# Two decoder layers on one core: projection weights fetched again, sums on VectorE, halos issued after turnings, the seventh chunk by seven products

## The chip, the core and the metric

One of the eight NeuronCores of a Trainium2 chip runs the whole program. The metric is the device time of one execution in microseconds (us). Engines: PE is TensorE (matmul), PEld its weight load, DVE is VectorE, ACT is ScalarE, POOL is GpSimd, SP is SyncE, which only issues DMAs here. All five run their own instruction list strictly in the order in which it was written.

## The reference, cut to what matters

```python
def _A_ref(x, wqkv, wo):             # attention: 32 heads of 18, window 8, dilation 2
    qkv = (x @ wqkv) -> q, k, v
    idx = pos[:, None] - arange(8) * 2           # keys s, s-2, ..., s-14
    logits = einsum("bhsd,bhswd->bhsw", q, k[idx]) * 18 ** -0.5     # masked where idx < 0
    return einsum("bhsw,bhswd->bhsd", softmax(logits), v[idx]) @ wo
def _B_ref(x, w1, w2):               # feed-forward, 576 -> 4608 -> 576
    return silu(x @ w1) @ w2
x = A_x                              # 2048 tokens x 576, f32
for _ in range(2):                   # the same weights in both layers
    x = x + _A_ref(layernorm(x), A_wqkv, A_wo)
    x = x + _B_ref(layernorm(x), B_w1, B_w2)
```

## The kernel before, in words

**Chunks.** The 2048 tokens are cut into four chunks of 512, and with two layers there are eight steps s = 0 to 7, "chunk s" below; chunks 4 to 7 are the second layer, and the seventh chunk is s = 6. Every f32 operand of a matmul is held as two f16 halves (high and low), so a product takes three matmuls. In the feed-forward, chunks 0 and 1 are computed plainly (`ffn`), chunks 2 to 7 in pairs of 128-row weight blocks (`ffn_pairs`): 18 pairs q, in six groups g of three.

**A pair.** Its first product x @ w1 is a 2x2 block product done with seven block products P1 to P7 instead of eight (`product`, L1199, seven matmuls of 128x256 each). For these the inputs are combined beforehand: `forms` makes sums of blocks of x (L1153), splits them (L1162 to L1168) and turns them by DMA transposes into `xf` (L1172). ACT and DVE take the results out of the four PSUM banks and add them up (L1203, L1206, L1226), and Silu follows. The second product with w2 is done in one of two ways. `second` (L1316) does it plainly: 48 matmuls of 128x288 a pair. `seconds` (L1289) does it by seven block products: 42 matmuls a pair. For these `hidden_forms` makes four sums a pair (L1253, on POOL) and splits them (L1258, L1261), and the weights must have been combined before by `prepare_second` (two loads L1095, four sums L1101 on POOL, a split on ACT L1103 and DVE L1104, a store L1106), once for each of the 18 pairs. `TWICE` says from which group on a chunk uses `seconds`: chunk 6 from group 2, chunk 7 from group 0.

**Attention of the second layer.** For each chunk, four units u of 8 heads: a load of wqkv's part (`load_wq`, 1080 KB, one buffer), 4 x 14 matmuls (L717), evacuation by ACT (L784, L786), and then the "halo": four DMAs on POOL's queue that copy the last rows of keys and values to the neighbour partition (L798). DVE computes scores and weighted sums (L818, L822, L851, L858). `project` then handles the chunk's four 128-token tiles j: DVE splits o, SP issues a DMA transpose ("turning", L496, `yo<-yh`, two buffers `yo`), PE multiplies by wo (L894, 28 matmuls), DVE adds the residual in place (L905) and POOL's queue writes it out (`xe<-o`, L899). `turn` later loads it again and makes the chunk's `forms`.

**Order.** The order of every instruction list is made when the program is built. The class `Plan` holds the operations with an assumed duration, a priority (`prio`, lower first), their dependencies (`after` adds some by hand) and their buffers; `order` plays them through with assumed DMA times (1.2 us before, 0.9 us after, and a rate) and writes each engine's list in the order in which that play started them. `AT`, `AN` and `AD` are priorities of the second layer's attention, so that its work lies among the matmuls of the chunk before. What the chip does when a DMA or an engine is later than in that play is wait.

**Areas.** `area` and `part` lay several kinds of tiles over the same bytes of SBUF; a tile can be taken when nothing that overlaps it is alive. The weights `wo` have a tile of their own throughout. The four sums `turn` makes of each half of a chunk (`ye`, `yd`) lie in the area of `xa` (turned normalized inputs of attention) or, for chunk 5, of `o` (attention's output).

## Time and profile before

| | |
|---|---|
| three runs, us | 2153.5, 2153.89, 2156.87; median 2153.89 |
| the profiled execution, us | 2151.35 |
| its span, first to last instruction, us | 2149.6 |
| PE busy | 2101.2 us, 98% |
| DVE, ACT, POOL busy | 1730.4 us (81%), 1014.7 us (47%), 540.6 us (25%) |
| granted clock of TensorE, mean | 0.996 |
| DMA | 482.00 MB, 224 GB/s |

A row of the windows view gives for a stretch of time the busy us of each engine with its number of instructions, the granted clock of TensorE, the busy share of the 16 DMA engines and GB/s. A row of the waits view gives who waited for whom: us in total, how often, the longest. A row of the chain or the timeline gives start, length and what ran; the timeline adds in brackets how long the engine had been idle before and who ended that. The chain's rows on a DMA run from its issue to its landing.

### The profile page before, as it was taken

What the parts mean: (1) busy time and instruction counts of PE and PEld (TensorE: products, weight loads), DVE (VectorE), ACT (ScalarE), POOL (GpSimd) and SP (SyncE); (2) the same over time, 40 slices, a digit from 0 to 9 for tenths busy, and PEclk for the clock granted to TensorE, in tenths of its full rate; (3) what the DMA queues carried; (4) which work ended last, traced back from release to release, by engine and by line L of the source; (5) the groups of instructions that cost most, each with busy time, mean ns of one, the idle gap of its engine ahead of it and who ended that gap; (6) DMA issues with size and microseconds to landing.
All of it is one profiled execution on the core that took longest, in us unless ns stands there. A gap on an engine that the chain in (4) does not pass through costs nothing.

```text
span 2149.6 us, 41975 instructions
## 1 busy us (share of the span) xinstructions
PE 2101.2 (98%) x16053; PEld 1560.2 (73%) x16053; DVE 1730.4 (81%) x2681; ACT 1014.7 (47%) x1851; POOL 540.6 (25%) x819
## 2 busy tenths in 40 slices
PE   8999899999999999999999999999999999999999
PEld 5556466655667888777777867778787887887887
DVE  8999999999978999789989968974997457555444
ACT  7555788654344553344324424424444454444443
POOL 2224656243332230111101000010002624222222
PEclk9999999999999999999999999999999999999999
DMA  6577777697889987687668986787769897979772
GB/s 181 156 224 253 253 259 252 171 273 250 230 200 285 323 260 217 165 249 194 172 190 206 268 204 194 212 185 201 221 174 252 308 294 243 281 205 270 209 208 76
DMA packets 372881, 482.00 MB, mean 224 GB/s; under 512 B 150072, under 2 KB 294820, under 8 KB 368712
## 3 DMA queue, kind: packets, MB, share of 16 engines
q1 hardware_dynamic: 327848, 331.25, 55.4%
q0 software_dynamic: 42816, 146.97, 21.2%
q8 instruction: 125, 2.05, 0.4%
q10 hardware_dynamic: 2016, 1.11, 0.2%
q14 instruction: 76, 0.62, 0.1%
HBM read 345.36 MB, written 85.37 MB: 200 GB/s over the span
## 4 chain that ended last, share of the span: by engine, by line
PE 79%; DMA 9%; DVE 7%; issue 3%; ACT 1%; POOL 1%; SPq 0%; ACTq 0%; DVEq 0%; POOLq 0%
PE acc L1316 19%; PE misc L1199 12%; PE z L1199 12%; PE z L717 8%; PE acc L1289 7%; PE z L1358 7%; PE acc L1377 6%; PE misc L717 5%; PE acc L894 4%; DMA yo<-yh 2%; DMA w<-w2s 1%; DMA w<-wfs 1%; DMA wq<-in_B_w_dram 1%; DVE xa L1067 1%; DVE x L905 1%
## 5 line engine op out<-in xcount | busy, mean ns | idle before, releaser
L1199 PEld LDWEIGHTS <-w 128*128 128x128 f16 x5292 | 517.8, 98 | 87.8 <-issue 11.6
L1316 PE MATMUL acc<-w,h 128*128 128x288 f16 x3744 | 484.0, 286 | 0.0
L1316 PEld LDWEIGHTS <-h 128*128 128x128 f16 x3744 | 366.1, 98 | 89.1
L1199 PE MATMUL misc<-xb,w 128*128 128x256 f16 x2639 | 338.5, 273 | 10.9 <-DMA w<-wfs 4.4
L1199 PE MATMUL z<-xb,w 128*128 128x256 f16 x2653 | 338.3, 273 | 4.2 <-ACT wq L1203 3.0
L1377 PE MATMUL acc<-w,h 128*128 128x288 f16 x1728 | 215.8, 286 | 2.2 <-DMA w<-w2s 2.2
L717 PEld LDWEIGHTS <-xa 128*128 128x128 f16 x1344 | 131.3, 98 | 116.9 <-issue 4.1
L1377 PEld LDWEIGHTS <-h 128*128 128x128 f16 x1728 | 168.4, 98 | 46.8 <-issue 2.6
L851 DVE TENSOR_TENSOR prs<-kvs,pe 128x1152 f32<-128x1152 f32 x128 | 169.9, 1350 | 0.8
L818 DVE TENSOR_TENSOR prs<-qts,kvs 128x2304 f32<-128x2304 f32 x64 | 163.2, 2550 | 4.0 <-DMA kvs<-kvs 3.0
L822 DVE TENSOR_REDUCE lg<-prs 128x128 f32<-128x2304 f32 x64 | 162.9, 2546 | 1.0
L905 DVE SCALAR_TENSOR_TENSOR x<-acc,d,x 128x576 f32<-128x576 f32 x144 | 116.4, 811 | 54.8 <-PE acc L1316 48.6
L858 DVE TENSOR_TENSOR prs<-prs 128x1152 f32<-128x1152 f32 (+1 forms) x128 | 135.0, 1055 | 3.2
L1358 PE MATMUL z<-xb,w 128*128 128x512 f16 x588 | 129.1, 379 | 4.3 <-ACT w L978 1.6
L1298 DVE SCALAR_TENSOR_TENSOR x<-acc,d2x,x 128x576 f32<-128x576 f32 (+1 forms) x71 | 57.3, 809 | 86.1 <-PE acc L1289 83.7
L894 PE MATMUL acc<-wo,yo 128*128 128x288 f16 x896 | 117.0, 291 | 8.7 <-DMA yo<-yh 7.3
L717 PE MATMUL z<-wq,xa 128*128 128x432 f16 x630 | 121.7, 349 | 2.9 <-DMA wq<-wqs 2.9
L894 PEld LDWEIGHTS <-yo 128*128 128x128 f16 x896 | 88.6, 99 | 35.4 <-DMA yo<-yh 9.2
L1358 PEld LDWEIGHTS <-w 128*128 128x128 f16 x588 | 57.2, 98 | 73.5 <-DVE w L980 2.9
L717 PE MATMUL misc<-wq,xa 128*128 128x432 f16 x546 | 105.0, 346 | 2.7 <-ACT xa L494 1.3
L798 POOL DMA_DIRECT2D kvs<-kvs x64 | 34.5, 545 | 271.3 <-ACT qts L786 271.3
L1358 PE MATMUL z<-xb,wq 128*128 128x512 f16 x420 | 94.5, 384 | 2.6 <-ACT h L1360 2.6
(302 smaller groups left out, 3227.3 us busy)
## 6 DMA issues: line engine op xcount, KB each, us to landing
w<-wfs SPq DMA_DIRECT2D x756, 160.0 KB
w<-w2s SPq DMA_DIRECT2D x192, 288.0 KB
wq<-wqs SPq DMA_DIRECT2D x17, 1080.0 KB
kvs<-kd POOLq DMA_DIRECT2D x8, 1584.0 KB, 10.3
w<-w1s SPq DMA_DIRECT2D x36, 320.0 KB
wfs<-xa POOLq DMA_DIRECT2D x18, 640.0 KB, 4.6
w2s<-w POOLq DMA_DIRECT2D x36, 288.0 KB, 4.2
kvs<-wts SPq DMA_DIRECT2D x67, 144.0 KB
```

The source lines that it names most:

```text
L717: nc.tensor.matmul(T(m)[:, :3 * UC], a, b, start=n == 0, stop=n == len(pl) - 1)
L818: nc.vector.tensor_tensor(T(pr), T(qt)[:, j:j + 2, None, :].to_broadcast([P, 2, W, UC]), win(T(kv), j, 2), op=ALU.mult)
L822: nc.vector.tensor_reduce(T(lg)[:, j:j + 2].rearrange("p a w h -> p (a w h)"), T(pr).rearrange("p a w (h d) -> p (a w h) d", d=DH), axis=A ...
L851: nc.vector.tensor_tensor(T(pr)[:, a].rearrange("p w (h d) -> p w h d", d=DH), v, T(pe)[:, j + a, :, :, None].to_broadcast([P, W, UH, DH]) ...
L858: nc.vector.tensor_tensor(t[:, :, 0:h, :], t[:, :, 0:h, :], t[:, :, h:2 * h, :], op=ALU.add)
L894: nc.tensor.matmul(T(acc)[:, h, 0:288], a, b[:, h * 288:(h + 1) * 288], start=n == 0, stop=n == len(pl) - 1)
L905: nc.vector.scalar_tensor_tensor(t, acc[:, :, 0:288], d, t, op0=ALU.mult, op1=ALU.add)
L1199: nc.tensor.matmul(t, w[:, u, :], v[:, r, :], start=first and m == 0, stop=m == 6, skip_group_check=True)
L1289: nc.tensor.matmul(T(acc)[:, j, 0:KH], T(hb[t])[:, a, row[k], j * P:(j + 1) * P], T(wb[k, t])[:, w, :], start=k in (5, 1, 2) and t == 0 an ...
L1316: nc.tensor.matmul(T(acc)[:, h, 0:288], T(hb[t])[:, a, f, j * P:(j + 1) * P], T(wbs[t][f])[:, h, w, :], start=t == 0 and f == 0 and m == 0 ...
L1358: nc.tensor.matmul(T(z), v, u, start=m == 0, stop=m == len(pl) - 1)
L1377: nc.tensor.matmul(T(acc)[:, h, 0:288], T(hb[q])[:, a, j * P:(j + 1) * P], T(wbs[q][0])[:, h, w, :], start=q == 0 and m == 0, stop=q == n ...
```

## The change

- `TWICE` has 0 for chunk 6: all its 18 pairs use `seconds`.
- The sums of `hidden_forms` and `prepare_second` go from POOL to DVE, with new assumed durations.
- The tile of `wo` becomes the area `wos`, which the sums `ye` share; `yd` is gone. The split weights are stored to memory once (in step 2), and fetched again (1440 KB, `load_wo`) for the projections of chunks 5 and 6, and again for that of chunk 7. Four dependencies by hand that kept `xa`, `o` and the sums apart go away.
- `free`: unit 1's matmuls and edges of chunks 5 to 7 must follow the last turning of the projection before, so its halo comes behind the turnings.
- `lag`: the planner takes it that matmuls of `project` (2.5 us) and of `product` (0.7 us) in the second layer can start so much after the DMA that they need.

```diff
-TWICE = {6: 2, 7: 0}
+TWICE = {6: 0, 7: 0}
+LAGP = 2.5
+LAGX = 0.7
...
-                t = max(t, d.end + (0.0 if d.eng == o.eng and not d.nbytes else self.LAT))
+                t = max(t, d.end + (0.0 if d.eng == o.eng and not d.nbytes else self.LAT) + (o.lag if d.nbytes else 0.0))
...
-    part("ye", XA, 1, [2, 4, KH], F32)
-    part("yd", O, 1, [2, 4, KH], F32)
-    tag("wo", 1, [P, 10, D], F16)
+    WOA = area("wos", 10 * D * 2)
+    part("wo", WOA, 1, [10, D], F16)
+    part("ye", WOA, 1, [2, 4, KH], F32)
...
+    def load_wo(prio):
+        w = Buf("wo")
+        op("SP", 0.41, lambda: nc.sync.dma_start(fl(T(w)), wos), ["wos"], [(w, k) for k in range(10)], prio, nbytes=P * 20 * D, after=formed[-1:])
+        return w
...
         for u in range(NU):
+            free = held[:1] + (flipped[-1:] if s > NC and u == 1 else [])
...
-                    op("SP", 0.8, edge, [("eds", lay, par, u)], [(kv, "edge")], pr_, nbytes=20000, lanes=2, after=held[:1])
+                    op("SP", 0.8, edge, [("eds", lay, par, u)], [(kv, "edge")], pr_, nbytes=20000, lanes=2, after=free)
...
-                           [m, (kv, "hold")] if lay else [m], pr_, after=held[:1])
+                           [m, (kv, "hold")] if lay else [m], pr_, after=free)
...
-                    op("DVE", 1.28, mul, keys + [pe], [(pr, a)], pd, after=formed[-1:] if s <= NC or s == NC + 3 else ())
+                    op("DVE", 1.28, mul, keys + [pe], [(pr, a)], pd, after=formed[-1:] if s <= NC else ())
...
-            transposed(oh, lambda oT=oT: T(oT), oT, j, pd, s < 2)
+            flipped.append(transposed(oh, lambda oT=oT: T(oT), oT, j, pd, s < 2))
...
-            op("PE", 3.43, mm, [(oT, j)] + [(WO, k) for k in range(10)], [acc], pr_)
+            op("PE", 3.43, mm, [(oT, j)] + [(w, k) for k in range(10)], [acc], pr_, lag=LAGP if s >= NC else 0.0)
...
-                nc.gpsimd.tensor_tensor(t[:, r], t[:, x], t[:, y], op=ALU.subtract)
-        op("POOL", 3.8, sums, [(b, 0)], [(b, 0)], prio)
+                nc.vector.tensor_tensor(t[:, r], t[:, x], t[:, y], op=ALU.subtract)
+        op("DVE", 1.85, sums, [(b, 0)], [(b, 0)], prio)
...
-                    return op("PE", 0.763, mm, [wf[k], (xf[k], 0), (xf[k], 1)], [z], pp + 0.01 * q)
+                    return op("PE", 0.763, mm, [wf[k], (xf[k], 0), (xf[k], 1)], [z], pp + 0.01 * q, lag=LAGX if s >= NC else 0.0)
...
-            op("POOL", 0.75, lambda hq=hq, r=r, u=u, v=v, o=o: nc.gpsimd.tensor_tensor(T(hq)[:, r], T(hq)[:, u], T(hq)[:, v], op=o),
+            op("DVE", 0.42, lambda hq=hq, r=r, u=u, v=v, o=o: nc.vector.tensor_tensor(T(hq)[:, r], T(hq)[:, u], T(hq)[:, v], op=o),
...
-                   [(yh, 0), (yh, 1), (xT, "hold")], p, nbytes=P * 9 * P * 2, after=formed[-1:] if s == NC + 2 else ())
+                   [(yh, 0), (yh, 1), (xT, "hold")], p, nbytes=P * 9 * P * 2)
...
     def attend(s):
-        project(s, attention(s, normed[s], lambda u: load_wq(u, AT[s], "wz")))
+        if s in (NC + 1, NC + 3):
+            outs.append(load_wo(AT[s]))
+        project(s, attention(s, normed[s], lambda u: load_wq(u, AT[s], "wz")), None, outs[-1])
 
     def turn(s):
-        XT[s] = forms(load_x(s, s - 1.0, spilt=True), s - 1.0, late=spilled[-1:] if s == NC + 1 else gate[-1:], into="yd" if s == NC + 1 else "ye")
+        XT[s] = forms(load_x(s, s - 1.0, spilt=True), s - 1.0, into="ye")
...
+        if s == 2:
+            op("POOL", 0.55, lambda: nc.gpsimd.dma_start(wos, fl(T(WO))), [(WO, k) for k in range(10)], ["wos"], 2.0, nbytes=P * 20 * D, after=attended[-1:])
```

Since the plan is played through anew, the lists differ from the third chunk (s = 2) on; up to there they are the same but for names. PE has 36 matmuls fewer. Three places follow; line numbers of the changed kernel are up to 10 higher (L496 is now L500, L663 L667, L798 L808, L887 L897, L899 L909, L915 L925, L1077 L1087, L1104 L1114).

**SP, the projection of chunk 6.** Before (L496 `yo<-yh` are the four turnings, L887 the residuals' loads, L663 a unit's weights, L1077 weights of `product`):

```order
L887 DMA o<-xd_110 128x576
L496 DMA_TRANSPOSE yo<-yh 128x9x128
L887 DMA o<-xd_111 128x576
L496 DMA_TRANSPOSE yo<-yh 128x9x128
L663 DMA wq<-wqs_252 128x4320
L887 DMA o<-xd_112 128x576
L496 DMA_TRANSPOSE yo<-yh 128x9x128
L887 DMA o<-xd_113 128x576
L496 DMA_TRANSPOSE yo<-yh 128x9x128
```

With the change:

```order
L897 DMA o<-xd_110 128x576
L500 DMA_TRANSPOSE yo<-yh 128x9x128
L1087 DMA w_70<-wfs_228 128x640
L897 DMA o<-xd_111 128x576
L500 DMA_TRANSPOSE yo<-yh 128x9x128
L1087 DMA w_70<-wfs_228 128x640 x2
L1087 DMA w_70<-wfs_229 128x640
L897 DMA o<-xd_112 128x576
L1087 DMA w_70<-wfs_229 128x640 x2
L500 DMA_TRANSPOSE yo<-yh 128x9x128
L897 DMA o<-xd_113 128x576
L500 DMA_TRANSPOSE yo<-yh 128x9x128
```

The load of the next unit's weights, which is issued when the matmuls of the unit before are done, stood between the second and the third turning; now all four turnings come first.

**POOL, the projection of chunk 5.** Before (L899 `xe<-o` writes out a projected tile, L798 is a halo's four DMAs):

```order
L899 DMA xe_122<-o 128x576
L899 DMA xe_123<-o 128x576
L899 DMA xe_124<-o 128x576
L798 DMA kvs<-kvs 112x1152
L798 DMA kvs<-kvs 15x1152
L798 DMA kvs<-kvs 112x864
L798 DMA kvs<-kvs 14x864
L899 DMA xe_125<-o 128x576
```

With the change:

```order
L909 DMA xe_122<-o 128x576
L909 DMA xe_123<-o 128x576
L909 DMA xe_124<-o 128x576
L909 DMA xe_125<-o 128x576
L808 DMA kvs<-kvs 112x1152
L808 DMA kvs<-kvs 15x1152
L808 DMA kvs<-kvs 112x864
L808 DMA kvs<-kvs 14x864
```

The halo of unit 1 of chunk 6 follows the last projected tile of chunk 5; the halo of unit 0 still stands ahead of `xe_122`, but the matmuls that it waits for come earlier on PE: between unit 0's last matmul and the projection's first stood 12 matmuls, and now 248.

**The sums of `prepare_second`.** Before, on POOL:

```order
L1101 TENSOR_TENSOR kvs<-kvs 128x288 x8
L1101 TENSOR_TENSOR prs<-prs 128x288 x4
L1106 DMA wts_232<-kvs 128x2304
L1106 DMA wts_233<-kvs 128x2304
L899 DMA xe_130<-o 128x576
```

With the change, on DVE (L1111 are the sums, L1114 the split, L915 the residual adds of L905 before):

```order
L1111 TENSOR_TENSOR kvs<-kvs 128x288 x4
L915 SCALAR_TENSOR_TENSOR o<-acc_98,so,o 128x576
L1111 TENSOR_TENSOR kvs<-kvs 128x288 x4
L1114 SCALAR_TENSOR_TENSOR kvs<-kvs,accw 128x4x288
L915 SCALAR_TENSOR_TENSOR x_75<-acc_99,d_307,x_75 128x576
L1114 SCALAR_TENSOR_TENSOR kvs<-kvs,accw 128x4x288
```

POOL has no arithmetic left there; DVE's list has the sums between its other work. On PE the projection of chunk 7 stands among the products of chunk 5's pairs 4 to 6 instead of its pairs 11 to 14, and in chunk 6 the first matmuls of `seconds` follow the last of chunk 5's `second`.

More of the change, by code (lines that the diff above doesn't have):

```diff
@@ L65 @@
 class Op:
-    __slots__ = ("eng", "dur", "fn", "prio", "seq", "deps", "outs", "n", "bufs", "nbytes", "start", "end", "table", "lanes")
+    __slots__ = ("eng", "dur", "fn", "prio", "seq", "deps", "outs", "n", "bufs", "nbytes", "start", "end", "table", "lanes", "lag")
 class Plan:
@@ L86, in slots, with op @@
         self.named[tag] = 0
-    def op(self, eng, dur, fn, reads=(), writes=(), prio=0.0, nbytes=0, table=None, after=(), lanes=1):
+    def op(self, eng, dur, fn, reads=(), writes=(), prio=0.0, nbytes=0, table=None, after=(), lanes=1, lag=0.0):
         o = Op()
+        o.lag = lag
         o.eng, o.dur, o.fn, o.prio, o.seq, o.nbytes, o.table = eng, dur, fn, prio, len(self.ops), nbytes, table
@@ L399, in sliding_attention_silu_ffn @@
     wts = [tc.dram_tile([P, 4 * 2 * KH], F16, name=f"wts{q}") for q in range(NP)]
+    wos = tc.dram_tile([P, 10 * D], F16, name="wosd")
     wqs = [tc.dram_tile([P, 30 * UC], F16, name=f"wqs{u}") for u in range(NU)]
@@ L507, in sliding_attention_silu_ffn @@
     attended, spilled, stored = [], [], []
-    turned, held = [], []
+    turned, held, flipped = [], [], []
     marks = []
@@ L770, in clear @@
                         nc.gpsimd.memset(T(kv)[0:1, 3:7], 0.0)
-                    op("POOL", 1.86, clear, [], [(kv, "edge")], pr_, after=held[:1])
+                    op("POOL", 1.86, clear, [], [(kv, "edge")], pr_, after=free)
                 else:
@@ L859, in tree @@
                     nc.vector.tensor_tensor(T(o)[:, j:j + 2, u * UC:(u + 1) * UC], t[:, :, 0, :], t[:, :, 1, :], op=ALU.add)
-                done = op("DVE", 2.55, tree, [], [(pr, 0), (pr, 1), (o, j, u), (o, j + 1, u)], pd, after=formed[-1:] if s <= NC or s == NC + 3 else ())
+                done = op("DVE", 2.55, tree, [], [(pr, 0), (pr, 1), (o, j, u), (o, j + 1, u)], pd, after=formed[-1:] if s <= NC else ())
                 if s == 0:
@@ L865, in attention, with project @@
         return o
-    def project(s, o, xs=None):
+    def project(s, o, xs=None, w=WO):
         pr_, pd = AT.get(s, s - 1.0), AD.get(s, s - 1.0)
@@ L887, in project @@
                 op("SP", 0.41, lambda j=j: nc.sync.dma_start(T(o)[:, j, :], xd[c][j]), [("xd", c, j)], src, pd, nbytes=P * D * 4)
-            transposed(oh, lambda oT=oT: T(oT), oT, j, pd, s < 2)
+            flipped.append(transposed(oh, lambda oT=oT: T(oT), oT, j, pd, s < 2))
             def mm(oT=oT, acc=acc):
-                pl = list(passes(lambda k: T(oT)[:, k, :], lambda k: T(WO)[:, k, :]))
+                pl = list(passes(lambda k: T(oT)[:, k, :], lambda k: T(w)[:, k, :]))
                 for n, (a, b) in enumerate(pl):
@@ L1459, in front @@
         XT[s] = layer_norm(X[s], s - 1.0, "xb", s == 1, s == 0) if s < S2 else forms(X[s], s - 1.0, ("ya", "yc"))
-    normed = {}
+    normed, outs = {}, [WO]
     def norm(s):
```

## The prediction

> **What bounds the kernel now.** I read the page first, then PE's waits, then stretches engine by engine, then the chain of waits around the longest gaps. The page's head:
>
> ```profile
> span 2149.6 us, 41975 instructions
> PE 2101.2 (98%) x16053; PEld 1560.2 (73%) x16053; DVE 1730.4 (81%) x2681; ACT 1014.7 (47%) x1851; POOL 540.6 (25%) x819
> ```
>
> PE is the bound: only 48.4 us of the span are not matmuls. So a change can gain in two ways, by fewer matmuls or by fewer gaps. The largest rows of PE's waits from 718 us to the end, in the part that the change reorders (up to about 580 us the lists are the same):
>
> ```profile
> PE acc L894 <- DMA yo<-yh: 7.3, 4, 2.9
> PE misc L1199 <- DMA w<-wfs: 4.4, 3, 3.5
> PE misc L1199 <- DVE wq L1206: 3.0, 2, 1.6
> PE z L1199 <- ACT wq L1203: 3.0, 2, 2.5
> PE z L717 <- DMA wq<-wqs: 2.9, 2, 2.7
> PE misc L1199 <- ACT wq L1203: 2.6, 3, 1.1
> ```
>
> That is 23.2 us in six rows. Most of the other idle time lies earlier and stays. A long gap costs twice, for after it the clock is lower. Windows right after gaps of 2.8, 1.5, 3.5, 2.5 and 2.9 us (PE, PEld, DVE, ACT, POOL, then the clock):
>
> ```profile
> 1436.20:1439.60 3.40, 3.40 (x16) 2.19 (x17) 0.88 (x1) 0.00 (x0) 0.00 (x0) 0.53 1.17 161
> 1087.40:1090.80 3.40, 3.40 (x29) 2.71 (x30) 0.59 (x1) 0.00 (x0) 0.00 (x0) 1.00 1.31 174
> 1977.20:1980.60 3.40, 3.39 (x29) 2.83 (x30) 0.63 (x2) 0.00 (x0) 0.32 (x1) 1.00 0.93 299
> 1804.60:1808.00 3.40, 3.40 (x19) 2.42 (x17) 3.40 (x10) 2.34 (x4) 0.38 (x1) 0.50 0.72 236
> 1275.20:1278.70 3.50, 3.50 (x17) 2.27 (x18) 3.46 (x4) 0.00 (x0) 0.00 (x0) 0.55 1.15 327
> ```
>
> After 1436 us 16 matmuls fit into 3.4 us where 29 fit after 1087 us: half the clock for 3.4 us, so 1.7 us lost on top of the gap.
>
> **The change part by part.**
>
> *Fewer matmuls.* Groups 0 and 1 of chunk 6 are six pairs; each needs 42 matmuls of 128x288 instead of 48, so 36 fewer. How fast they follow each other is in the chain of waits, which also has the turnings of the next part:
>
> ```profile
> 1050.11 5.88 PE acc L1316 x48
> 1072.26 3.43 PE acc L894 x28
> 1097.32 0.76 PE misc L1199 x7
> 831.47 7.22 DMA yo<-yh
> 1075.72 11.58 DMA yo<-yh
> 1258.65 16.47 DMA yo<-yh
> 1423.95 12.19 DMA yo<-yh
> 912.68 11.46 DMA wq<-wqs
> ```
>
> 5.88 / 48 = 0.1225 us, times 36: **-4.4 us**. PE is full in that stretch, so it counts.
>
> *Halos behind turnings.* Four turnings make one projection. One with no halo near it landed after 7.2 us; the three on which PE waited longest took 11.6, 16.5 and 12.2 us. Each time a halo was issued within 3 us of them on POOL's queue:
>
> ```profile
> 1073.09 2.12 POOL L798 DMA_DIRECT2D kvs<-kvs  x4 [11.83 <-ACT qts L786]
> 1259.08 2.13 POOL L798 DMA_DIRECT2D kvs<-kvs  x4 [14.93 <-ACT qts L786]
> 1421.02 2.11 POOL L798 DMA_DIRECT2D kvs<-kvs  x4 [21.52 <-ACT qts L786]
> DMA to landing us min/median/max: 4.5/9.3/13.8
> ```
>
> (The last row is of all halos: they move for 9.3 us.) What covers a turning can be counted. There are two `yo` buffers, so tile 2's turning is issued when tile 0's matmuls are done. In chunk 6's projection 28 matmuls of L894, 42 of L1199 and 12 of L1316 stood between those and tile 2's, which is 3.4 + 4.6 + 1.5 = 9.5 us; 12.2 less 9.5 is 2.7, and PE waited 2.8. In the changed list the covers of tile 2 in the four projections come to 10.8, 9.5, 9.4 and 9.4 us, about as before; but no halo and no unit's weight load stands among the turnings any more, so 7.2 us should do. Then the 7.3 us go, and with them the two spells at half the clock after 1275 and 1436 us: **-7.3 - 3.4 = -10.7 us**. The bounds: if only the halos of unit 1 were to blame (1073 and 1421 us), 1.5 + 2.8 + 1.7 = 6.0; if other transfers delay the turnings as much, nothing. I take the whole, since all three places are rid of both.
>
> The Trainium skill ("TensorE: Matmul & The Clock Gate", section "HAM oscillation — how this bites in real kernels") has it that only PE gaps above about 3.4 us are punished. By that the gaps of 2.8 and 2.9 us would cost no clock and this term would be -7.3. The rows above say otherwise in both directions: half the clock after 2.5 to 2.9 us, the full clock after 3.5.
>
> *Sums on DVE.* Most of the waits on L1203 and L1206 fall into the time from 1622 to 1818 us, in which POOL makes the sums of `prepare_second`. PE's waits from 1600 to 1810 us beside the row on L1206 above, one of them in the timeline, and one source line:
>
> ```profile
> PE z L1199 <- ACT wq L1203: 2.5, 1, 2.5
> PE misc L1199 <- ACT wq L1203: 2.1, 2, 1.1
> 1785.24 3.41 POOL L1101 TENSOR_TENSOR o<-o 128x288 f32<-128x288 f32 x4
> 1790.01 0.93 PE L1199 MATMUL misc<-xb,w 128*128 128x256 f16 x7 [1.63 <-DVE wq L1206]
> L522 DVE TENSOR_TENSOR nt<-nt x34: 160/161/646, 8.0 to 1787.2; 128x4 f32<-128x4 f32 x30, 128x2 f32<-128x2 f32 x4
> ```
>
> A step that takes 0.16 us elsewhere takes 0.65 on DVE at 1787 us, while POOL works; so DVE comes late to the adds in its list, PSUM banks stay full, and PE waits. With POOL's arithmetic gone DVE runs at its own pace: 3.0 + 2.5 + 2.1 and the spell after 1804 us, **-7.6 - 1.7 = -9.3 us**; the other bound is 0, if DVE is late by its own work. For it gets 72 sums of 128x288 and 144 of 128x256 (24 of them new, for the six pairs). Such a sum was not on DVE; its nearest rows are an add of that shape with one input in PSUM, 0.417 us, and POOL's own 0.725. I take the first, as the same engine's, and a ninth more for the larger, 0.46:
>
> ```profile
> L1206 DVE TENSOR_TENSOR wq<-misc,wq x90: 377/417/425, 923.0 to 2113.8; 128x256 f32<-128x256 f32 x90
> L1253 POOL TENSOR_TENSOR wq<-wq x80: 716/725/887, 1813.6 to 2117.4; 128x256 f32<-128x256 f32 x80
> 900.00:1550.00 650.00, 638.58 (x4964) 486.78 (x4963) 546.75 (x791) 252.89 (x499) 66.40 (x112) 0.99 0.78 210
> 1550.00:1850.00 300.00, 290.70 (x2455) 240.59 (x2454) 206.71 (x304) 132.68 (x240) 93.50 (x118) 0.99 0.83 248
> 1850.00:2145.00 295.00, 289.91 (x2497) 243.65 (x2496) 149.19 (x220) 125.12 (x227) 77.20 (x110) 1.00 0.71 205
> ```
>
> 72 x 0.46 + 144 x 0.417 = 93 us, all behind the attention of chunk 7 and so nearly all after 1550 us, where DVE has 93 + 146 = 239 us free: cost on the path 0. At POOL's price it would be some 160 us, which fits too.
>
> *Attention of chunk 7 earlier.* DVE has 103 us free between 900 and 1550 us. The part of chunk 7's attention that came after 1550 us now moves in:
>
> ```profile
> L851 DVE TENSOR_TENSOR prs<-kvs,pe 128x1152 f32<-128x1152 f32 x8 | 10.6, 1350 | 0.1
> L858 DVE TENSOR_TENSOR prs<-prs 128x1152 f32<-128x1152 f32 (+1 forms) x10 | 10.6, 1055 | 0.3
> L818 DVE TENSOR_TENSOR prs<-qts,kvs 128x2304 f32<-128x2304 f32 x4 | 10.2, 2551 | 0.1
> L822 DVE TENSOR_REDUCE lg<-prs 128x128 f32<-128x2304 f32 x4 | 10.2, 2547 | 0.1
> 750.00:800.00 50.00, 50.00 (x431) 41.91 (x430) 48.40 (x62) 24.20 (x40) 20.01 (x29) 1.00 0.85 263
> ```
>
> That is 42 us, with the smaller steps of softmax an estimated 47: DVE goes from 84% to 91% there. Chunk 7's projection waits behind its list, and behind that on PE everything. Between 750 and 800 us DVE was busy 97% and PE did not wait at all (last row), so I count 0; the bounds are 0 and 47.
>
> *Waits on `w<-wfs`*, 4.4 us. The planner puts 0.7 us before each product, and the 38 weight tiles for chunk 6's first `seconds` are fetched well ahead of its start instead of in a burst at it. Of 0 to -4.4 I take half: **-2.2**. The wait on `wq<-wqs` of 2.7 us was an 11.5 us load that 77 products covered; now 84 cover it, 0.8 us more, which leaves 1.9, between gaps that cost clock (2.5) and one that did not (1.5). Between 0 and -2.5 I take **-1.0**.
>
> *The loads of `wo`*: 2 x 1440 KB on SP. A unit's 1080 KB took at worst the 11.5 us above; a third more is 15. They stand some 50 us of matmuls ahead of their projections, with weights for 12 products already fetched: 0. One store and two loads in 482 MB.
>
> *New waits.* A new list brings its own small misses. What I leave of the six rows (half of `wfs`, the rest of `wqs`, 1.0 of L1203) is some 5 us over 1430; the bounds are 0 and 25, as many as before. I take **+7**.
>
> Sum: -4.4 - 10.7 - 9.3 - 2.2 - 1.0 + 7 = -20.6 us. The profiled execution's 2151.4 us (its span and 1.8 around it) become 2130.8; the median of the runs is 2.5 above it, so **2133 us**.
>
> **The rivals.**
>
> *The turnings stay late.* If it is not the halos but the DMA load as such (the 16 engines are busy 78% from 900 to 1550 us), PE keeps these 10.7 us and the gaps on `wfs` and `wqs`, with 3 of new waits: -4.4 - 9.3 + 3 = -10.7, **2143 us**. For it: a unit's weight load also stood among the turnings, and loads are added. Against it: 7.2 us at 831 us, in slices of the page as busy with DMA.
>
> *As many new waits as old ones.* +25 in place of +7 gives -2.6, **2151 us**, no change. For it: the six rows came about in a list that was planned in the same way. Against it: four of the six lose their cause.
>
> *VectorE runs out before chunk 7's projection.* DVE's 103 us were free because it waited for halos, turnings and sums; where those waits stay, the 47 us do not fit. PE then stands at L894, with the rest of chunk 5 queued behind. The gains without new waits are 27.6 us, so it decides from 28 of the 47 on: with 36 it is **2162 us**, slower. Against it: chunk 7's attention waited by hand for chunk 5's forms, and that is gone.
>
> The Trainium skill ("Perfetto Trace Analysis", section "Optimizing Scalar/DVE Operations") speaks for this last rival: it would take work from a saturated VectorE to GpSimd, not back. The same section warns that the two share a port, so that it might not help, which the 0.65 us bear out.
>
> **How the numbers follow.** Forecast 0.60, turnings 0.14, no change 0.13, VectorE 0.13. The forecast's own range is 2122 (nothing new, all of `wfs` and `wqs` gained: -31.3) to 2146 (half of the turnings and of the sums, and +10: -7.6). For 8 in 10 I leave out VectorE's case and the upper half of no change: 2122 to 2152. A difference of 0.2%, 4.3 us, is about what a measurement of this kernel can tell from none. Faster: 0.60 + 0.14 = 0.74; same 0.13; slower 0.13.
>
> **What would show it.** Right: 36 matmuls fewer; no row L894 <- DMA `yo<-yh`, and turnings of 4 to 8 us; no waits of L1199 on L1203 or L1206 above 1 us after 1550 us, and L522 at 0.16 us throughout; half the clock after at most two gaps past 718 us; DVE at 88 to 94% from 900 to 1550 us. Wrong: a wait of PE at L894 on DVE or on `wos`, or PE's waits on DMA past 718 us above 10 us.

## The result, and the profile after

| | before | changed |
|---|---|---|
| runs, us | 2146.94 to 2156.87, median 2153.89 (5) | 2129.74 to 2138.56, median 2133.81 (5) |
| the profiled execution, us (span) | 2151.35 (2149.6) | 2134.51 (2132.7) |
| half-clock spells of PE past 600 us | 924, 1275, 1436, 1804 us | 641, 722 us |

The change is faster by 20.1 us: ratio 0.991, 95% interval 0.9886 to 0.9933. The two profiled executions are 16.9 us apart. The head of the changed kernel's page:

```profile
span 2132.7 us, 41915 instructions
PE 2093.9 (98%) x16017; PEld 1554.6 (73%) x16017; DVE 1811.8 (85%) x2909; ACT 1025.3 (48%) x1857; POOL 388.7 (18%) x628
```

PE's busy time is 7.3 us less, about what 36 matmuls (4.4 us) and two half-clock spells of 1.7 us come to. Where its idle time went is seen by windows, first of the kernel before, then of the changed one (length, then busy us of PE, PEld, DVE, ACT, POOL, clock, DMA share, GB/s):

```profile
0.00:718.00 718.00, 700.54 (x4597) 438.12 (x4597) 664.08 (x1081) 423.59 (x735) 276.82 (x441) 1.00 0.76 233
718.00:2150.00 1432.00, 1400.61 (x11458) 1122.06 (x11456) 1066.35 (x1601) 591.09 (x1116) 263.80 (x378) 1.00 0.78 220
```

```profile
0.00:718.00 718.00, 696.87 (x4552) 434.24 (x4553) 656.58 (x1071) 420.59 (x729) 269.97 (x432) 1.00 0.76 232
718.00:2133.00 1415.00, 1397.05 (x11468) 1120.34 (x11465) 1155.20 (x1839) 604.69 (x1128) 118.77 (x196) 1.00 0.80 228
900.00:1550.00 650.00, 643.15 (x5006) 488.61 (x5005) 590.22 (x837) 263.65 (x522) 69.08 (x117) 1.00 0.79 216
```

Past 718 us PE was idle 1432.00 - 1400.61 = 31.4 us before and 18.0 us now; ahead of 718 us it lost 3.7 us (21.1 against 17.5). So -7.3 - 13.4 + 3.7 = -17.0. The waits of PE in the changed kernel: six of the eleven rows past 718 us, and then those from 580 to 718 us:

```profile
PE misc L1209 <- DMA w<-wfs: 3.0, 3, 1.7
PE acc L1299 <- DVE h L1271: 2.0, 2, 1.6
PE z L1209 <- DVE wq L1216: 1.9, 2, 1.2
PE misc L1209 <- DVE wq L1216: 1.3, 2, 0.7
PE z L1209 <- DMA w<-wfs: 1.2, 2, 0.6
PE misc L1209 <- ACT wq L1213: 0.5, 1, 0.5
```

```profile
PE z L1368 <- ACT h L1370: 4.0, 1, 4.0
PE acc L904 <- DMA yo<-yh: 1.8, 1, 1.8
```

The rows on `yo<-yh` (7.3 us) and on `wq<-wqs` (2.9) are gone past 718 us, and those of the products (L1209) on ACT's and DVE's evacuation (L1213, L1216) past 1500 us are down from 7.6 to 1.0 us. In their place came 2.0 us on VectorE's splits for `seconds` (L1271), and two waits at 601 and 641 us, ahead of the stretch that the prediction looked at. The second costs clock as well, as does a short pair at 722 us; the one at 601 us does not:

```profile
640.80:644.20 3.40, 3.39 (x9) 1.17 (x9) 2.39 (x4) 3.39 (x6) 0.00 (x0) 0.51 1.15 334
722.60:726.00 3.40, 3.40 (x17) 2.14 (x15) 2.24 (x4) 0.38 (x1) 1.15 (x2) 0.51 0.93 289
600.00:604.00 4.00, 3.25 (x27) 2.61 (x28) 2.70 (x3) 3.44 (x5) 0.23 (x1) 1.00 1.07 296
```

The sums on VectorE, and the small steps of `newton` that had taken 0.65 us beside POOL's work:

```profile
L1111 DVE TENSOR_TENSOR kvs<-kvs x40: 445/457/459, 1574.8 to 1684.1; 128x288 f32<-128x288 f32 x40
L1263 DVE TENSOR_TENSOR wq<-wq x96: 370/419/427, 1747.8 to 2102.4; 128x256 f32<-128x256 f32 x96
L526 DVE TENSOR_TENSOR nt<-nt x34: 160/161/164, 7.9 to 1781.1; 128x4 f32<-128x4 f32 x30, 128x2 f32<-128x2 f32 x4
```

Each sum costs what was estimated (0.46 and 0.417), and every small step takes 0.16 us. One thing in the first row was not foreseen: the sums of `prepare_second` now end at 1684 to 1693 us; before they ran from 1622 to 1819 us.

### The profile page after: what moved, and what is told of

Read it like the earlier page. It is cut to its first block, busy times and chain, and to the rows that moved or that the text cites. A ratio compares the mean times of both kernels' runs of the same rounds, so it can differ in the third digit from the quotient of the medians.

```text
span 2132.7 us, 41915 instructions
## 1 busy us (share of the span) xinstructions
PE 2093.9 (98%) x16017; PEld 1554.6 (73%) x16017; DVE 1811.8 (85%) x2909; ACT 1025.3 (48%) x1857; POOL 388.7 (18%) x628
## 4 chain that ended last, share of the span: by engine, by line
PE 62%; DMA 7%; DVE 5%; issue 3%; POOL 0%; ACT 0%; SPq 0%; DVEq 0%; POOLq 0%; ACTq 0%
PE acc L1326 17%; PE z L1209 12%; PE misc L1209 11%; PE acc L1299 9%; PE z L726 3%; PE acc L904 3%; PE misc L726 3%; PE acc L1387 3%; PE z L1368 2%; DMA w<-wfs 2%; DMA w<-w2s 1%; DMA wq<-in_B_w_dram 1%; DMA xb<-yo 1%; DVE prs L828 1%; DVE lg L832 1%
## 5 line engine op out<-in xcount | busy, mean ns | idle before, releaser
L1209 PEld LDWEIGHTS <-w 128*128 128x128 f16 x5292 | 516.7, 98 | 82.4 <-issue 8.9
L1326 PE MATMUL acc<-w,h 128*128 128x288 f16 x3456 | 448.7, 287 | 1.4 <-DVE h L1247 0.9
L1326 PEld LDWEIGHTS <-h 128*128 128x128 f16 x3456 | 338.3, 98 | 86.4 <-DVE h L1247 1.8
L1209 PE MATMUL z<-xb,w 128*128 128x256 f16 x2695 | 341.7, 273 | 3.9 <-DVE wq L1216 1.9
L1209 PE MATMUL misc<-xb,w 128*128 128x256 f16 x2597 | 331.5, 273 | 5.4 <-DMA w<-wfs 3.0
L1387 PE MATMUL acc<-w,h 128*128 128x288 f16 x1728 | 215.4, 286 | 1.1 <-DMA w<-w2s 1.1
L1387 PEld LDWEIGHTS <-h 128*128 128x128 f16 x1728 | 168.3, 98 | 45.6 <-issue 1.5
L915 DVE SCALAR_TENSOR_TENSOR x<-acc,d,x 128x576 f32<-128x576 f32 x136 | 110.1, 811 | 41.8 <-PE acc L1326 35.2
L1308 DVE SCALAR_TENSOR_TENSOR x<-acc,d2x,x 128x576 f32<-128x576 f32 (+1 forms) x85 | 68.8, 810 | 68.5 <-PE acc L1299 68.4
L904 PE MATMUL acc<-wos,yo 128*128 128x288 f16 x896 | 113.7, 286 | 3.0 <-DMA yo<-yh 1.8
L1299 PEld LDWEIGHTS <-h 128*128 128x128 f16 x924 | 90.2, 98 | 24.0 <-DVE h L1271 2.6
L904 PEld LDWEIGHTS <-yo 128*128 128x128 f16 x896 | 87.4, 98 | 27.1 <-DMA yo<-yh 2.3
L726 PE MATMUL misc<-wq,xa 128*128 128x432 f16 x518 | 100.1, 346 | 2.7 <-ACT xa L498 1.3
```

The costliest lines, as they stand in the source:

```text
L726: nc.tensor.matmul(T(m)[:, :3 * UC], a, b, start=n == 0, stop=n == len(pl) - 1)
L904: nc.tensor.matmul(T(acc)[:, h, 0:288], a, b[:, h * 288:(h + 1) * 288], start=n == 0, stop=n == len(pl) - 1)
L915: nc.vector.scalar_tensor_tensor(t, acc[:, :, 0:288], d, t, op0=ALU.mult, op1=ALU.add)
L1209: nc.tensor.matmul(t, w[:, u, :], v[:, r, :], start=first and m == 0, stop=m == 6, skip_group_check=True)
L1299: nc.tensor.matmul(T(acc)[:, j, 0:KH], T(hb[t])[:, a, row[k], j * P:(j + 1) * P], T(wb[k, t])[:, w, :], start=k in (5, 1, 2) and t == 0 an ...
L1326: nc.tensor.matmul(T(acc)[:, h, 0:288], T(hb[t])[:, a, f, j * P:(j + 1) * P], T(wbs[t][f])[:, h, w, :], start=t == 0 and f == 0 and m == 0 ...
```

## The experiments

The kernels ran in three groups of four, each group on one chip with the kernel before beside it (medians 2156.2, 2153.7 and 2152.9 us). The first group has the two with one transfer moved, the one without sums and the one with the sums of `prepare_second` back on POOL; the second those without the rule, without the lags, with chunk 6 as it was and with the sums of `hidden_forms` on POOL; the third the rest.

### One transfer moved: halos, or unit loads

Two kernels made from the one before. Only POOL's list differs in the first, only SP's in the second:

```diff
-    for o in S.order():
+    made = S.order()
+    for what, behind in ((("halo", 5, 1), ("out", 4, 3)), (("halo", 7, 1), ("out", 6, 3))):
+        o = lab[what]
+        made.remove(o)
+        made.insert(made.index(lab[behind]) + 1, o)
+    for o in made:
```

In the second its third line is this one:

```diff
+    for what, behind in ((("load", 3.2, 2), ("turn", 4, 3)), (("load", 3.4, 2), ("turn", 6, 3))):
```

Here `lab` holds the planned operations by kind, chunk (or priority) and unit or tile; the first moves the halos of unit 1 of chunks 5 and 7 behind the last tile that is written out, the second the loads of their unit 2 behind the fourth turning. Halos moved:

> The kernel before, its lists unchanged but for POOL's: the halos of unit 1 of chunks 5 and 7 stand behind the last written tile of the projection that they stood in. Theory (halos delay the turnings): tile 2's turnings in the projections of chunks 4 and 6 land after 5 to 7 us in place of 11.6 and 12.2; PE's waits at L894 on yo<-yh fall from 7.3 us to about 3 (chunk 5's stays), and one spell at half the clock goes: about 6 us shorter than the kernel before. Rival (the load of the next unit's weights, which stays among the turnings, delays them): 11 to 12 us again, PE's waits 7.3, no time gained.

Loads moved:

> The kernel before, its lists unchanged but for SP's: the 1080 KB loads of unit 2's weights of chunks 5 and 7 stand behind the fourth turning of the projection that they stood in; the halos stay. Theory (halos): tile 2's turnings still take 11 to 12 us, PE's waits on yo<-yh stay at about 7 us. Rival (the load): they land after 5 to 7 us, PE's waits fall to about 3, 6 us shorter. If both count, something like 8 to 9 us for the turnings and half of the wait in either run.

Measured: 2149.9 and 2145.9 us, one run each, against a median of 2156.2 us (2154.7 to 2160.9) for the kernel before beside them. How long the four turnings of a projection took, in us from the issue to the last of its 16 semaphore events in the trace (the bottom row is an experiment further down):

```
                chunk 4 (tiles 0 to 3)      chunk 5                     chunk 6
before          3.99  3.65 11.58  9.64      4.17 16.47 13.86  3.54      5.82  5.40 12.19 11.49
halos moved     3.69  3.74  4.10  4.64      4.23 17.32 14.25  5.35      5.84  5.16  5.44  3.76
loads moved     3.80  4.12  6.47  4.79      4.12 16.95 14.14  3.90      6.21  5.68  6.78  4.92
changed         4.91  6.65  4.59  4.11      4.88  4.25  5.50  3.56      4.48  3.97  3.39  3.75
no free rule    3.60  3.86 14.55  8.55      3.77  3.88 10.07 11.09      3.79  3.81  7.81  4.77
```

In both kernels the chunks with the moved transfer (4 and 6) are cured, and chunk 5, where nothing was moved, stays late. PE's waits on turnings past 718 us, with the halos moved and with the loads moved:

```profile
PE acc L895 <- DMA yo<-yh: 3.7, 2, 3.4
```

```profile
PE acc L895 <- DMA yo<-yh: 4.2, 2, 3.7
```

One wait of 3.4 and 3.7 us is left of each, the one of chunk 5. So in these two places neither the halo alone nor the 1080 KB load alone made a turning late, and taking away either was enough. For the first kernel the theory's numbers came, for the second its rival's. This is not a rule on turnings in general. In the changed kernel the fourth turning of chunk 2 took 13.2 us (from 587.5 us) with neither beside it, but with seven raw weight loads issued on POOL's queue from 587.0 to 591.3 us; that is the wait at 601 us. In both kernels chunk 5's late turnings lay beside unit 0's halo and unit 1's load, which the rule on unit 1 does not move; in the changed list they were issued some 20 us ahead of that projection's first turning.

### Without the rule on unit 1

```diff
-            free = held[:1] + (flipped[-1:] if s > NC and u == 1 else [])
+            free = held[:1]
```

> The changed kernel without the rule that unit 1's matmuls follow the last turning of the projection before. In this list unit weights (1080 KB) stand again between the second and the third turning of chunk 4's projection, and halos come ahead of the projected tiles on POOL's queue; the plan gives third tiles 15.5, 12.3, 9.5 and 11.1 us of cover in chunks 4 to 7. Theory, as the two kernels with one transfer moved have left it (a turning is late only with a unit's load and a halo both in flight): some turning of chunks 4 to 7 takes over 9 us here, and PE waits on yo<-yh for 1 us or more at chunk 6 or 7, where the cover is smallest; 2135 to 2143 us. Rival: with POOL's sums gone, turnings are on time whatever stands beside them: all under 8 us, no such row, 2134 us as the changed kernel.

Measured: 2148.2 us (10 runs, 2142.7 to 2151.6), ratio 0.9985 (0.9967 to 1.0004): nearly all of the gain is lost, more than either theory allowed. The turnings are late again (14.6 us in chunk 4, 10.1 and 11.1 in chunk 5), though not quite as the theory has it: the one of 14.6 us was issued at 1091.4 us, when the unit's load had landed for 1.5 us, and the halo and five loads of w2 were still in flight. PE waits elsewhere than expected. The largest rows past 718 us, and then VectorE's timeline in front of the wait of 2.8 us at 1293.6 us:

```profile
PE misc L1209 <- DMA w<-wfs: 5.4, 2, 2.8
PE acc L904 <- DMA w<-w2s: 2.8, 1, 2.8
PE z L1209 <- DMA xb<-yh: 2.5, 1, 2.5
```

```profile
1286.05 1.28 DVE L1247 SCALAR_TENSOR_TENSOR h<-wq,sh,h 128x1024 f16<-128x1024 f32 x1
1292.63 0.82 DVE L1141 BATCH_NORM_STATS2 st<-x 128x6 f32<-128x288 f32 x2 [5.31 <-DMA x<-xe]
1295.75 0.77 DVE L915 SCALAR_TENSOR_TENSOR o<-acc,so,o 128x576 f32<-128x576 f32 x1
```

The row names a DMA that L904 does not need; its turning had landed at 1291.0 us. VectorE's list shows what it did need: a PSUM bank, which the residual add L915 set free at 1296.5 us. That add stood behind L1141, which waited 5.3 us for `x<-xe`, the projected tile that POOL's queue writes out behind the halo and SP loads again behind the turnings. The crowd of transfers delays more than the turnings. Since this kernel's lists were planned anew, the 14 us are those of the rule and of what the list made of it.

### Without the planner's lags

```diff
-LAGP = 2.5
-LAGX = 0.7
+LAGP = 0.0
+LAGX = 0.0
```

> The changed kernel with both assumed lags at 0. The matmuls that stand ahead of a third tile's (behind the first tile's) in the projections of chunks 4 to 7 come to 11.0, 8.7, 8.0 and 8.6 us of work instead of 10.8, 9.5, 9.4 and 9.4, ahead of a fourth tile's to 6.4, 6.4, 10.5 and 9.4 instead of 8.9, 9.8, 9.4 and 9.4. If it is halos and unit weight loads that make a turning late, and both are still behind the four turnings here, turnings land in 3 to 7 us and PE waits for none of them by more than 0.7 us; what comes back is waits on w<-wfs, up to 4 us: 2134 to 2138 us. Rival: the planner's lag is what removed the waits; then rows of L904 on DMA yo<-yh of 2 us or more come back with a spell of half the clock behind each, and the time is 2140 us or more.

Measured: 2140.4 us (10 runs, 2129.2 to 2144.5), ratio 0.994 (0.992 to 0.9961). Past 718 us:

```profile
PE misc L1209 <- DMA w<-wfs: 3.2, 5, 1.2
PE z L1209 <- DMA w<-wfs: 2.3, 3, 1.2
PE z L1209 <- DMA xb<-yo: 2.1, 1, 2.1
PE acc L904 <- DMA yo<-yh: 1.2, 1, 1.2
```

The wait on a turning is in chunk 3, and those of chunks 4 to 7 take 3.3 to 7.0 us without a wait. So it was not the lag that cured the turnings; what comes back is short waits on `wfs` (5.5 us against 4.2) and on the forms. The median is above the range that was expected, by less than its uncertainty of some 4 us; by the time alone it would be the rival's (2140 or more), but the rows and spells that the rival named for chunks 4 to 7 did not come.

### The sums: left out, on POOL, on VectorE, in either list

Left out, in the kernel before; and back on POOL, in the changed kernel's list:

```diff
-            t = four()
-            for r, x, y in ((0, 1, 0), (1, 3, 1), (3, 3, 0), (2, 2, 3)):
-                nc.gpsimd.tensor_tensor(t[:, r], t[:, x], t[:, y], op=ALU.subtract)
+            pass
...
-                nc.vector.tensor_tensor(t[:, r], t[:, x], t[:, y], op=ALU.subtract)
+                nc.gpsimd.tensor_tensor(t[:, r], t[:, x], t[:, y], op=ALU.subtract)
```

> The kernel before without the four sums of prepare_second on POOL (72 instructions less on POOL, all else in place): the second product of chunks 6 and 7 works on weights that were not combined. Theory (POOL's sums slow DVE down): a step of L522 takes at most 0.2 us, PE's waits of L1199 on L1203 and L1206 from 1600 to 1820 us fall from 7.6 to under 2 us, one spell at half the clock goes, about 9 us shorter. Rival (DVE is late by its own list): the waits stay above 5 us, at most 2 us shorter.

> The changed kernel, all lists planned as there, with the four sums of prepare_second made by POOL at the places that they have in the plan. Theory: DVE's small steps take up to 0.65 us again while POOL works, PE's waits on L1213 and L1216 after 1500 us rise from 0.9 to 4 to 9 us; 4 to 9 us slower than the changed kernel, 2138 to 2143. Rival (DVE's added work costs as much as it saves): within 2 us of the changed kernel, or faster.

Measured: 2140.6 us without the sums (one run, span 2138.8, 10.8 less than before), and all waits on ACT and DVE past 1600 us gone but 1.3 us. That is as the theory had it, and the kernel before ran at 2156.2 us beside it. The sums put back on POOL in the changed list cost little: 2137.6 us (4 runs, 2134.7 to 2143.7), ratio 0.9916 (0.989 to 0.9941), with 3.8 us of waits on L1213 and L1216 past 1500 us against 1.0. The small steps, which no longer lie beside the sums, stayed at 0.16 us. So the other half was tried, the sums on VectorE in the old list:

```diff
-                nc.gpsimd.tensor_tensor(t[:, r], t[:, x], t[:, y], op=ALU.subtract)
+                nc.vector.tensor_tensor(t[:, r], t[:, x], t[:, y], op=ALU.subtract)
```

> The kernel before, its lists as they were, but the 72 sums of prepare_second are done by VectorE at the same places. If it was POOL's arithmetic that slowed VectorE, and the new list adds nothing to that, the gain is that of leaving the sums out, 10.8 us in the one execution, less what 72 x 0.457 us of sums cost VectorE on the path (0 to 3): 2143 to 2147 us; waits of L1199 on L1203 and L1206 past 1600 us under 2 us. Rival: VectorE is late there by its own work; then the sums put 33 us more ahead of its adds, such waits stay at 5 us or grow, and the time is 2153 us or more.

Measured: 2151.5 us (10 runs, 2148.3 to 2156.1), ratio 0.9994 (0.9978 to 1.0009): no gain at all. Its rows on the small steps, on the sums, and PE's waits past 1600 us:

```profile
L522 DVE TENSOR_TENSOR nt<-nt x34: 160/162/165, 8.0 to 1788.0; 128x4 f32<-128x4 f32 x30, 128x2 f32<-128x2 f32 x4
L1101 DVE TENSOR_TENSOR kvs<-kvs x40: 448/457/459, 1625.6 to 1803.4; 128x288 f32<-128x288 f32 x40
PE z L1199 <- ACT wq L1203: 4.8, 2, 4.5
PE misc L1199 <- DVE wq L1206: 1.9, 2, 1.3
```

The small steps are fast, and the wait is still there, larger than before (4.5 us at 1806 us). What ACT waited for ahead of it, in the kernel before and in this one, and the windows from 1780 to 1805 us of the two:

```profile
1802.29 0.44 ACT L1162 ACTIVATE yo<-xa 128x288 f16<-128x288 f32 x1 [4.34 <-DVE xa L1153]
1780.00:1805.00 25.00, 20.88 (x179) 17.33 (x177) 23.98 (x41) 11.26 (x23) 14.79 (x19) 0.99 0.66 221
```

```profile
1804.22 0.44 ACT L1162 ACTIVATE yo<-xa 128x288 f16<-128x288 f32 x1 [5.29 <-DVE xa L1153]
1780.00:1805.00 25.00, 21.06 (x179) 17.27 (x177) 23.61 (x57) 9.32 (x18) 1.07 (x2) 0.98 0.73 252
```

ACT's split for `forms` stands ahead of L1203 in ACT's list and waits for a sum of `forms` (L1153) on VectorE, which is full: 24.0 and 23.6 of 25 us. In those 25 us lie the layer norm and the sums of chunk 7's `forms`, residual adds, and the splits of `prepare_second`. VectorE's list is the same in the three kernels but for the sums, so its steps can be compared one by one. Ahead of that L1153, from 1780 us on, stand 36 of them: 22.1 us of work in the kernel before, 15.9 us without the sums, and 15.9 us with the sums on VectorE. What stands just before it, first in the kernel before, then with the sums on VectorE:

```profile
1798.99 2.31 DVE L1148 TENSOR_SCALAR x<-x,mv,nt 128x576 f32<-128x576 f32 x2
```

```profile
1800.91 1.06 DVE L1148 TENSOR_SCALAR x<-x,mv,nt 128x576 f32<-128x576 f32 x2
1801.88 1.94 DVE L1101 TENSOR_TENSOR kvs<-kvs 128x288 f32<-128x288 f32 x4
```

So POOL's sums cost VectorE 6.3 us there by slowing its steps, and on VectorE they cost it 7.3 us as four groups of their own. Either way PE loses 4 us; with neither, the wait is gone. The changed list has no sums of `prepare_second` in that stretch any more (they end at 1693 us), and PE loses nothing. The stretch that answers to it, and that in which the sums now lie, first in the changed kernel, then with the sums of `prepare_second` back on POOL in its list:

```profile
1774.00:1799.00 25.00, 25.00 (x220) 21.28 (x219) 22.80 (x51) 12.32 (x26) 0.00 (x0) 1.00 0.74 212
1574.00:1694.00 120.00, 120.00 (x1036) 101.08 (x1034) 94.51 (x163) 59.47 (x93) 11.22 (x21) 1.00 0.96 322
```

```profile
1574.00:1694.00 120.00, 117.17 (x1006) 98.09 (x1005) 70.50 (x87) 57.30 (x91) 78.92 (x89) 1.00 0.93 307
```

There the engine makes a difference of 2.8 us. The waits of the products on ACT's and DVE's evacuation past 1500 or 1600 us put the four cases side by side: 7.6 us with the sums on POOL in the old list, 6.7 on VectorE in the old list, 3.8 on POOL in the new list, 1.0 on VectorE in the new list. In the old place the other engine takes away almost nothing; the new place takes away half with POOL and nearly all with VectorE (the two lists differ in more than this place). As to this experiment's two theories: POOL does slow VectorE, but the sums' own price on VectorE's path was 7.3 us in one stretch where 0 to 3 were allowed for, and the time came out near the rival's (2153 or more).

### The other sums, and all of them, on POOL in the new list

The four sums of `hidden_forms` alone, then these and those of `prepare_second`:

```diff
-            op("DVE", 0.42, lambda hq=hq, r=r, u=u, v=v, o=o: nc.vector.tensor_tensor(T(hq)[:, r], T(hq)[:, u], T(hq)[:, v], op=o),
+            op("DVE", 0.42, lambda hq=hq, r=r, u=u, v=v, o=o: nc.gpsimd.tensor_tensor(T(hq)[:, r], T(hq)[:, u], T(hq)[:, v], op=o),
```

> The changed kernel, same lists but for this: the 144 sums of hidden_forms are POOL's again (the other sums stay on VectorE). Theory: VectorE's waits came from the 72 larger sums of prepare_second, 13.6 us of POOL at a stretch, not from these, which come four at a time; and VectorE has over 100 us free past 1550 us either way. So the same time as the changed kernel within 3 us, with PE's waits on L1213 and L1216 past 1500 us below 4 us in all. Rival: any arithmetic on POOL slows VectorE's steps; 144 x 0.725 = 104 us of it would bring back 3 to 8 us of such waits: 2137 to 2142 us.

> The changed kernel, its lists as they are, with all 216 sums back on POOL. With the sums of prepare_second alone there, 2.5 us of short waits came and no spell of half the clock; with those of hidden_forms alone the time was within what can be told. Theory (contention, and the waits add up): 4 to 8 us above the changed kernel on this chip. Rival: in the new list POOL's sums no longer collide with VectorE's small steps and cost nothing, so that the gain I put down to the engine came from the list: within 2 us of the changed kernel.

Measured: 2140.1 us (10 runs), ratio 0.9936 (0.9915 to 0.9957), and 2141.7 us (6 runs), ratio 0.9948 (0.9919 to 0.9978). In the first the waits on L1213 and L1216 past 1500 us came to 1.9 us, as the theory had it, while the time fits its rival. The changed kernel itself ran beside the second:

> The changed kernel once more, beside the three others and the kernel before on one chip, so that differences of 2 to 6 us between its variants are read on the same chip. Ratio 0.991 as before, some 2134 us where the kernel before takes 2154. Rival: the ratio itself differs from chip to chip; then 2138 us or more, and the 2140 us of the kernels with one part undone were no loss.

It took 2138.6 us (6 runs, 2131.7 to 2140.2), ratio 0.9923 (0.9897 to 0.9948): 14.4 us less than the kernel before on that chip, where the first measurement had 20.1. The rival's number came (2138 or more), and the two ratios agree within their intervals. All sums on POOL are 3.1 us above it, between what theory and rival allowed and within the uncertainty. By the medians the engine's part cannot be told: the ratios with sums on POOL (0.9916, 0.9936 and 0.9948) overlap with the changed kernel's (0.991 and 0.9923). By the stretch of `prepare_second` it can, since PE's list is the same there in all of these kernels and in the one of the next section: for the matmuls that the changed kernel runs from 1574 to 1694 us, PE needs 120.1 us in each of the four executions with these sums on VectorE, and 123.5 and 123.1 us in the two with them on POOL. For the sums of `hidden_forms` nothing of the kind is shown.

### Chunk 6 as it was

```diff
-TWICE = {6: 0, 7: 0}
+TWICE = {6: 2, 7: 0}
```

> The changed kernel with one part undone: chunk 6 uses seven products only from its third group on, as before the change. PE gets 36 matmuls more; by the sum of the prediction that is 36 x 0.1225 = 4.4 us more than the changed kernel, so some 2138 us beside its 2133.8, with PE's busy time 4 to 5 us up and its waits past 718 us as in the changed kernel within 3 us. The covers of the second pair of turnings in the projections are the same to 0.1 us in both lists. Rival: the six pairs' seven products cost more than they save, by 24 sums on VectorE and by 37 loads on SP's queue; then this kernel is as fast as the changed one or faster.

Measured: 2144.4 us (10 runs, 2134.4 to 2148.7), ratio 0.9959 (0.9936 to 0.9982). That is 6 us above what was expected, and by the ratios 8 to 11 us above the changed kernel. Up to 1720 us all lists are the same, so the stretch behind tells most. From the same product at 1548 us (1542 us in the changed kernel) to the end, here and in the changed kernel:

```profile
1548.13:2144.60 596.47, 585.85 (x5044) 492.87 (x5043) 390.00 (x707) 261.05 (x467) 16.31 (x30) 1.00 0.78 233
```

```profile
1542.48:2132.70 590.22, 581.69 (x5008) 489.09 (x5007) 408.92 (x743) 265.46 (x473) 16.31 (x30) 1.00 0.81 240
```

36 matmuls and 4.2 us of PE more, and 2.1 us of gaps more: 6.3 us. The 4.4 us are there, and the sums and loads that buy them cost nothing on the path. The other 5.6 us between the two executions lie ahead of 1548 us, where the lists are the same: so far do executions of one list drift apart. What the medians differ by beyond 4.4 us is not explained. On the same chip this kernel is 4.3 us above the one with the sums of `hidden_forms` on POOL.

### A version to beat both

```diff
-            op("PE", 3.43, mm, [(oT, j)] + [(w, k) for k in range(10)], [acc], pr_, lag=LAGP if s >= NC else 0.0)
+            op("PE", 3.43, mm, [(oT, j)] + [(w, k) for k in range(10)], [acc], pr_, lag=LAGP if s >= NC else 5.0 if s == 2 else 0.0)
...
-                   [(f, 0), (f, 1)], [(x, a)], prio, nbytes=P * KB * 4)
+                   [(f, 0), (f, 1)], [(x, a)], prio, nbytes=P * KB * (4 if formed else 8))
...
-                    return op("PE", 0.763, mm, [wf[k], (xf[k], 0), (xf[k], 1)], [z], pp + 0.01 * q, lag=LAGX if s >= NC else 0.0)
+                    return op("PE", 0.763, mm, [wf[k], (xf[k], 0), (xf[k], 1)], [z], pp + 0.01 * q, lag=LAGX if s >= 2 else 0.0)
```

> A version to beat both. The planner's assumptions of lateness are carried into the first layer, where the changed kernel's largest gaps are left: the 0.7 us ahead of products from chunk 2 on, 5 us ahead of the projection's matmuls in chunk 2, and twice the transfer time for the turnings of the first forms (so that ACT's list puts less of them ahead of L1370). Theory: the gaps of 1.8 at 601, 4.0 at 641 and 2.3 us at 720 go, and the two spells of half the clock behind 641 and 722 (1.7 each): 11.4 us less than the changed kernel, with 3 us of new waits some 2126 us. Rival: the turning at 588 us is so late by other transfers (13 us) and the list so different behind it that as many new waits come: 2134 us.

Measured: 2135.6 us (4 runs, 2133.2 to 2137.7), ratio 0.9916 (0.9884 to 0.9948), against 2138.6 for the changed kernel on the same chip: not to be told from it. The gaps at 601, 641 and 720 us are gone, and two others stand in their place; PE's waits from 580 to 730 us, and VectorE in front of the second:

```profile
PE z L1209 <- DVE h L1216: 4.1, 1, 4.1
PE misc L1209 <- DVE xb L1216: 3.1, 1, 3.1
```

```profile
696.41 2.55 DVE L832 TENSOR_REDUCE lg<-prs 128x128 f32<-128x2304 f32 x1
699.00 2.56 DVE L828 TENSOR_TENSOR prs<-qts,kvs 128x2304 f32<-128x2304 f32 x1
701.48 2.08 DVE L1062 TENSOR_TENSOR wq<-wq 128x384 f32<-128x384 f32 x4
703.48 0.75 DVE L1216 TENSOR_TENSOR xb<-misc,xb 128x256 f32<-128x256 f32 x2
```

VectorE does long attention steps without a pause there, and the adds that free PSUM come behind them. It is the same pattern as at 1780 us in the old list: the rival of this run, new waits for old ones.

## Why the prediction held, step by step

The time (2133 us) and its sign came out; of the causes behind the sum one was half right and one was right only together with the new place of the sums, and sizes that were off offset each other. That the median lies within 1 us of the forecast is luck: the profiled pair gained 16.9 us, and the same kernel on another chip 14.4.

- **Fewer matmuls, -4.4.** Right: 36 fewer, and 4.2 us of PE when they are put back.
- **Turnings, -10.7.** The size is right: no wait on a turning past 718 us, turnings of 3.2 to 6.7 us, both spells gone. The cause, "halos behind turnings", is half of it. The prediction named the load of a unit's weights beside the halo but carried only the halo into its bound of 6.0; the runs show that in chunks 4 and 6 it took both, and that moving either away is enough. The wider bound of "if other transfers delay the turnings as much, nothing" did not come into play because the change moves both.
- **Sums on DVE, -9.3.** The gain is there: waits on ACT's and DVE's evacuation past 1500 us fell by 6.6 us, with one spell of 1.7. Its reason, that POOL's work makes DVE late to its adds, is right for the old list: the same 36 steps took 22.1 us beside POOL's sums and 15.9 without. What was too weak is the price on the path, "0" because DVE has 239 us free past 1550 us. Free time over 600 us says nothing of the 25 us in which the wait arises: in the old list the sums cost DVE 7.3 us there, and the whole gain was lost. The price came to 0 in the new list, which makes the sums ahead of chunk 7's `forms`; the prediction did not mention that. In the new place the engine alone was worth 2.8 us. What the Trainium skill says on this ("SBUF — State Buffer", section "Who interferes with whom") agrees with the rows on the small steps: a VectorE instruction with two inputs in SBUF contends with a GpSimd one that reads SBUF.
- **Attention of chunk 7 earlier, 0.** Right: DVE went to 590.2 of 650 us, 91% as worked out, and the projection of chunk 7 never waited for it.
- **`w<-wfs`, -2.2.** From 5.6 to 4.2 us in this execution, -1.4; in the repeated one 5.9 us, nothing. Without the lag 5.5. Sized too high.
- **`wq<-wqs`, -1.0.** Sized too low, with too narrow a bound (-2.5): the wait of 2.7 us and its spell of 1.7 both went, -4.4. The prediction counted 0.8 us more cover; the load itself landed in 6.2 us instead of 11.5.
- **Loads of `wo`, 0.** Right; they landed after 8.0 and 7.0 us, half of the 15 that were allowed for, and no matmul waited for them.
- **New waits, +7.** Too low: the terms above come to -4.4 - 10.7 - 8.3 - 1.4 - 4.4 = -29.2 as measured, and the spans differ by 16.9, so 12 us are new. 8.1 of them lie at 601 to 726 us (gaps of 1.8 and 2.9 more, two spells of 1.7): the prediction looked past 718 us alone, though the lists differ from 580 us on.

The signs that the prediction named for "right" came: 36 matmuls fewer, no wait on a turning past 718 us, no wait on evacuation above 1 us past 1550 us, small steps of 0.16 us, one half-clock spell past 718 us, DVE at 91%; some turnings were even faster than the 4 to 8 us that it named.

Of the rivals, "the turnings stay late" and "VectorE runs out" did not come. "As many new waits as old ones" was nearer than its 0.13: 12 of the 25 us came.

The rule that the prediction weighed ("TensorE: Matmul & The Clock Gate", section "HAM oscillation — how this bites in real kernels", in the Trainium skill: only gaps above some 3.4 us cost clock) does not hold here: half the clock followed gaps of 2.5 to 2.9 us that the change removed, and one of 1.7 us shortly behind another of 0.6 in the changed kernel. By that rule the term on turnings would have been 3.4 us smaller. What does decide over these spells the traces show; it is worked out at the end.

## What to carry to other kernels

An experiment that leaves work out shows what the work costs where it stands; it does not say whether the engine, the place or the amount is to blame. Move it to the other engine in the same list, and back in the new list, and compare how long the same instructions take beside it and without it, before you name the cause. Idle time averaged over hundreds of microseconds does not show that an engine can take more work in the few where a wait arises. Where a planner makes the lists, a small change to its costs moves work by 50 us or more: look at where the work now lies, not only at what it now costs. And when a transfer comes late, take away each of its neighbours alone: here, in two places, two were needed, and either could go.
